# One PSUM tile per bank, mixing in halves, and a new order in an attention and feed-forward kernel

## The chip, the cores and the metric

The kernel runs on one core of a Trainium2 chip. The metric is the device time of one execution in microseconds (us), here as the median of the timed runs. A core has TensorE (PE, matrix products, with its weight loads in a row of their own, PEld), VectorE (DVE), ScalarE (ACT), GpSimd (POOL) and SyncE (SP, which issues every DMA of this kernel). Matrix products are written to PSUM, which has eight banks of 512 float32 columns on 128 partitions; DVE and ACT read them from there.

## The reference, cut to what matters

```python
def _attn_ref(q, k, v):                       # q, k, v: (8, 12, 448, 64) float32
    S = q.shape[2]
    scores = matmul(q, k.transpose(0, 1, 3, 2)) / sqrt(64) - log(S)
    attn = 1 / (1 + exp(-scores))             # sigmoid attention, no row sum
    return matmul(attn, v)

def _moe_ref(x, U, V, w_ch1, w_ch2):          # x: (8, 448, 768); U: (448, 32); V: (32, 448)
    h = x.transpose(0, 2, 1) @ U @ V          # mixing along the sequence, rank 32
    u = x + h.transpose(0, 2, 1)
    return u + maximum(u @ w_ch1, 0) @ w_ch2  # w_ch1: (768, 3072); w_ch2: (3072, 768)
```

The 12 heads of 64 features side by side make the 768 columns of `x`. U, V and both weights arrive as 64-bit words that the kernel decodes itself.

## The kernel before, in words

**Data.** Everything is kept with features on partitions. A batch of `x` or `u` is six tiles of 128 x 448, one for each pair of heads: `ua0..5` or `ub0..5` in the profile's names. A matrix product that must be exact to float32 is made of three float16 products: each operand is scaled and split into a high and a low half, and high*high, high*low and low*high are added up in one bank.

**Attention** (`pair`). For batches 0 and 1 it is done in float32, for 2 to 7 in split float16. A pair of heads has four key blocks (the numbers 3, 0, 1, 2; block 3 is half a block for each head). `scores_of` (L500) makes the scores of two blocks at a time; ACT takes the sigmoid (L587), then writes the high half (L610); DVE makes the low half (the helper `rest`, L358); `values_of` (L511, L515) multiplies by v; ACT evacuates the result to `ub` (L616), and `largest` (L421) takes its largest value for the next scale. Ahead of each pair its q, k and v are loaded, their bounds taken on ACT (L415) and spread by two small DMAs (`far`, `row`).

**Mixing** (`mix`). After its six pairs a batch is mixed. For batches 2 to 7 all six tiles get one scale (`scale_max`, with two small products on PE, L371 and L377), are split into the tile `us` (ACT and POOL the high, DVE the low halves), turned by two transposing DMAs into `xt` (L664), multiplied by U (L673, seven products for three tiles), evacuated by ACT and DVE to the tile `xnt` (L648 and L358), multiplied by V (L728, six products), and added to `ub` by DVE. Then the six tiles are stored to DRAM (`parked`), and the next batch of attention may overwrite `ub`.

**Feed-forward.** Batches 0 to 3 go through it plainly, in six groups of 512 hidden columns. `ffn_in` (L823) is a chain of 18 products, which ACT evacuates twice (L830 to `r`, L831 to `h`) and DVE once more (L832, low half). `ffn_out` (L843) is a chain of 12 products, whose sum DVE adds to `ua` (L358). Weights are decoded in the first batch (`decode`: DVE passes over the words, ACT bounds, ACT or POOL high halves, DVE low halves; for the last quarter of the weights of all groups but the first, the low half is made by ACT and POOL instead, L791 and L792) and kept in DRAM (`scratch`); later batches load them. Attention of the later batches is laid between these chains. Batches 4 to 7 go through it in two pairs at the end (L1016), with seven products of quarter blocks in place of eight: `in_quad` and `out_quad`, twelve of each for a pair of batches, 63 products each, in the order that the string `ORDER` gives. The sums of weight quarters for it are made on POOL all along (L902, L906).

**Order.** Nothing is scheduled on the chip. `Plan.op` collects each operation with its engine, its assumed cost, a due time (`pos`) and the tiles it reads and writes. `Plan.order` runs a list of events over them: whichever engine is free first takes the operation with the earliest due time among those that can start. The instructions are emitted in that order, each engine runs its own in that order, and the layer below sets semaphores between them. The due times hang on the tuned numbers at the top of the file. SP issues its DMAs in order too; each takes the next of eight semaphores.

**PSUM.** The banks are made as four tiles of two banks each; the plan gives them out bank by bank, and scores as whole tiles:

```python
BANKS = [Buffer(ps.tile([P, 2, 512], F32, name=f"banks{i}")) for i in range(4)]
BANK = [Buffer(x.ap[:, i]) for x in BANKS for i in range(2)]
PF, PS_ = [BANK[:4]] + [BANK[:3]] * (B - 1), [BANK[4:]] * 2 + [BANK[3:]] * (B - 2)
```

`PF[b]` are the banks of the feed-forward of batch b and of the small products of the scales, `PS_[b]` those of attention and mixing of batch b. So from batch 1 on the feed-forward has banks 0 to 2, and from batch 2 on attention and mixing have banks 3 to 7. Banks 2 and 3 are the two halves of the tile `banks1`.

## Time and profile before

| | |
|---|---|
| median of 3 runs | 1673.56 us (1671.91 to 1676.96) |
| profiled execution, time and span | 1673.21 us, 1671.4 us |
| PE busy | 1576.5 us (94%) |
| DVE busy | 1121.8 us (67%) |
| ACT busy | 837.9 us (50%) |
| POOL busy | 402.4 us (24%) |
| DMA | 322.52 MB, mean 193 GB/s |

The span runs from the first to the last instruction; the time has 1.8 us more around it. Busy times are sums without overlap. PE's is that of matrix products; its idle time is the rest of the span. In rows of the timeline, the bracket at the end gives the engine's idle time just before the row and the instruction that ended it. Names lose their buffer number in the profile, so that `banks` is any of the four PSUM tiles.

### The profile page before, as it was taken

Reading aid. Unit: us, or ns where it says so; the run is one execution under the profiler, and the core shown is the slowest. Engines: PE = TensorE matmul, PEld = TensorE weight load, DVE = VectorE, ACT = ScalarE, POOL = GpSimd, SP = SyncE. Lnnn points to the kernel's source line nnn. Section 1 sums busy time; section 2 is a strip of 40 time slices with the busy share of each in tenths; the row PEclk is TensorE's granted clock in tenths of the full one; section 3 lists DMA queues with packets and bytes.
Section 4 is the critical chain, followed back from the end, with each engine's and each line's share of the span. In section 5 each row is a group of like instructions: output and inputs, shape, how many; then the busy total and the mean of one; then the engine's idle time right before and its main releaser. Section 6 shows DMA issues by size and latency. Waiting matters only on the chain.

```text
span 1671.4 us, 23667 instructions
## 1 busy us (share of the span) xinstructions
PE 1576.5 (94%) x8756; PEld 768.8 (46%) x8756; DVE 1121.8 (67%) x1829; ACT 837.9 (50%) x1431; POOL 402.4 (24%) x484
## 2 busy tenths in 40 slices
PE   8989998999989999989979999999899999999998
PEld 3344444444444444444434444445455544545554
DVE  3788787666765566656657775685869687464745
ACT  6757665568647547737748765132324344130310
POOL 0100103542213443211312210065656150000000
PEclk9999999999999999999989999999999999999999
DMA  8698877675765777574665746986667574333321
GB/s 253 231 296 269 277 261 228 227 232 137 176 177 147 213 228 201 135 217 136 158 167 164 191 158 202 266 253 207 212 205 234 226 254 150 125 107 104 127 100 66
DMA packets 217428, 322.52 MB, mean 193 GB/s; under 512 B 132832, under 2 KB 183392, under 8 KB 205024
## 3 DMA queue, kind: packets, MB, share of 16 engines
q1 hardware_dynamic: 217312, 321.01, 61.9%
q8 instruction: 68, 1.11, 0.3%
q14 instruction: 48, 0.39, 0.1%
HBM read 249.40 MB, written 77.42 MB: 196 GB/s over the span
## 4 chain that ended last, share of the span: by engine, by line
PE 71%; DVE 12%; issue 5%; DMA 5%; ACT 4%; POOL 2%; SPq 1%; DVEq 0%; POOLq 0%; ACTq 0%
PE banks L1016 30%; PE banks L823 14%; PE banks L843 14%; PE banks L500 6%; PE banks L515 4%; PE banks L511 2%; DVE a L358 1%; DVE stg__109 L358 1%; DVE us__87 L358 1%; DMA w<-w_in 1%; DMA y_out<-ua__79 1%; POOL stg__109 L355 1%; SPq L335 1%; ACT junk L415 1%; ACT at L587 1%
## 5 line engine op out<-in xcount | busy, mean ns | idle before, releaser
L843 PE MATMUL banks<-h__93,w__91 128*128 128x448 f16 x864 | 176.8, 358 | 14.2 <-ACT ub__81 L616 8.5
L843 PE MATMUL banks<-h__94,w__92 128*128 128x448 f16 x864 | 176.4, 358 | 9.0 <-ACT r__96 L830 2.8
L358 DVE SCALAR_TENSOR_TENSOR a<-at,a 128x896 f16<-128x896 f32 (+1 forms) x145 | 143.1, 1009 | 50.6 <-ACT a L610 50.3
L823 PE MATMUL banks<-us__87,w__89 128*128 128x448 f16 x648 | 129.9, 356 | 8.0 <-ACT r__95 L830 2.8
L843 PEld LDWEIGHTS <-w__91 128*128 128x128 f16 x864 | 83.0, 99 | 102.6 <-issue 31.6
L823 PE MATMUL banks<-us__87,w__90 128*128 128x448 f16 x648 | 127.5, 353 | 1.8 <-ACT inv_x__199 L384 1.1
L843 PEld LDWEIGHTS <-w__92 128*128 128x128 f16 x864 | 83.2, 99 | 95.1 <-issue 23.6
L823 PEld LDWEIGHTS <-w__89 128*128 128x128 f16 x864 | 83.6, 98 | 92.9 <-issue 18.1
L823 PEld LDWEIGHTS <-w__90 128*128 128x128 f16 x864 | 83.0, 98 | 86.6 <-issue 10.7
L610 ACT ACTIVATE a<-at 128x896 f16<-128x896 f32 (+1 forms) x144 | 116.9, 851 | 0.5
L1016 PEld LDWEIGHTS <-w__89 128*128 128x128 f16 x819 | 80.1, 98 | 76.7 <-issue 2.1
L1016 PEld LDWEIGHTS <-w__91 128*128 128x128 f16 x756 | 73.9, 98 | 76.3 <-issue 8.0
L1016 PEld LDWEIGHTS <-w__90 128*128 128x128 f16 x756 | 73.9, 98 | 74.5 <-issue 6.2
L906 POOL TENSOR_TENSOR w<-w 128x384 f32<-128x384 f32 x96 | 105.3, 1097 | 5.9
L1016 PEld LDWEIGHTS <-w__92 128*128 128x128 f16 x693 | 68.2, 98 | 72.5 <-issue 11.0
L902 POOL TENSOR_TENSOR w<-w 128x384 f32<-128x384 f16 x64 | 67.0, 1063 | 124.9 <-DVE xnt L910 76.2
L909 ACT CAST xnt<-w 128x1536 f16<-128x1536 f32 x24 | 35.3, 1469 | 64.6 <-POOL w L906 60.3
L587 ACT ACTIVATE at<-banks,bias_s,c__221 128x896 f32<-128x896 f32 (+1 forms) x60 | 56.0, 947 | 16.5 <-DVE a L358 9.7
L587 ACT ACTIVATE at<-banks,bias_s,c__222 128x896 f32<-128x896 f32 (+1 forms) x60 | 56.1, 946 | 8.4 <-PE banks L500 6.9
L587 ACT ACTIVATE at<-banks,bias_s,c__220 128x896 f32<-128x896 f32 (+1 forms) x60 | 55.7, 946 | 5.3 <-PE banks L500 4.7
L830 ACT ACTIVATE r__96<-banks 128x448 f32<-128x448 f32 x48 | 26.0, 542 | 60.2 <-PE banks L823 24.3
L830 ACT ACTIVATE r__95<-banks 128x448 f32<-128x448 f32 x48 | 26.0, 541 | 55.4 <-PE banks L823 29.6
(1194 smaller groups left out, 3152.6 us busy)
## 6 DMA issues: line engine op xcount, KB each, us to landing
w<-w_in SPq DMA_DIRECT2D x48, 768.0 KB, 5.7
forms<-xnt SPq DMA_DIRECT2D x24, 768.0 KB, 4.4
w__89<-forms SPq DMA_DIRECT2D x13, 1344.0 KB, 6.4
w__90<-forms SPq DMA_DIRECT2D x12, 1344.0 KB, 5.9
w__91<-forms SPq DMA_DIRECT2D x12, 1344.0 KB, 6.0
w__92<-forms SPq DMA_DIRECT2D x11, 1344.0 KB, 5.9
forms<-scratch SPq DMA_DIRECT2D x144, 96.0 KB, 4.1
w__89<-scratch SPq DMA_DIRECT2D x9, 1536.0 KB, 7.3
```

Source lines behind the costliest of these rows:

```text
L358: nc.vector.scalar_tensor_tensor(out=out, in0=in0, scalar=s, in1=in1, op0=op0, op1=op1)
L500: nc.tensor.matmul(o, keys, y[rows_of(h)], start=i == 0, stop=i == n - 1)
L515: nc.tensor.matmul(av.x[rows_of(h), :S], x[:, j, rows_of(h)], y(tiles[j], h), start=False, stop=j == 2 and i == n - 1, skip_group_check=True,)
L587: act(cost, lambda: nc.scalar.activation(out_(), in_(), AF.Sigmoid, bias=bias_s[rows], scale=c if whole else c.x[rows]), kin + ["bias"] + ...
L610: act(0.57 if j == 3 else 0.95, lambda a=a, to=to: nc.scalar.activation(half(a, 0), to.x, AF.Copy, scale=A_UP), kto, [(a, 0)], here)
L823: nc.tensor.matmul(ph.x[:, :S], wx[:, x, c, f * P : (f + 1) * P], us.x[:, c, y, :], start=c == 0 and i == 0, stop=c == NP - 1 and i == 2,)
L830: act(0.54, lambda: nc.scalar.activation(r.x, ph.x[:, :S], AF.Relu, scale=DOWN_H), [ph], [r], pos - 4)
L843: nc.tensor.matmul(po.x[:, :S], wx[:, x, f, e * P : (e + 1) * P], h.x[:, f, y, :], start=f == 0 and i == 0, stop=f == FC - 1 and i == 2,)
L902: pool(1.0, lambda j=j: nc.gpsimd.tensor_tensor(out=t.x[:, j], in0=quarter(j, 0), in1=quarter(j, 1), op=ALU.add), [(w, j, 0), (w, j, 1)] i ...
L906: pool(1.0, lambda o_=o_, x=x, y=y, sub=sub: nc.gpsimd.tensor_tensor(out=t.x[:, o_], in0=t.x[:, x], in1=t.x[:, y], op=ALU.subtract if sub ...
L909: act(1.45, lambda: nc.scalar.copy(o.x[:, :, :, 0], t.x.rearrange(order)), [(t, j) for j in range(4)], [(o, 0)], pos)
L1016: nc.tensor.matmul(bank.x[:, :S], wt.x[:, k, FACTOR[n], x], both(f)[:, y], start=start and k == i == 0, stop=k == 2 and i == 2, skip_group ...
```

## The change

Nine things are changed. (1) PSUM is eight tiles of one bank. (2) The scores of a block take two of these tiles, one for each head, from all the banks of attention (before: a two-bank tile of `banks2` or `banks3`, for all but the first pairs), and each gets a sigmoid of its own: two of 448 columns where one of 896 stood. (3) Batches 2 to 7 are mixed in halves of three tiles by the new function `mix_half`, one half after the third pair and one after the sixth, each with its own scale, its own tile `xs` for the split halves (before: one of the two `us` tiles that the feed-forward reads too) and its own `th` (before: a half of one `xnt` tile); there is one `xt` tile in place of two, and the stores to `parked` of three tiles follow each half. (4) `Plan.order` lets a DMA start only when the one eight before it has landed. (5) `LOW_POOL` is empty: the low halves that ACT and POOL made in `decode` are made by DVE. (6) `largest` of batch 1 is on DVE, no longer on ACT. (7) `ORDER` has in and out alternating. (8) The far sums of `far_forms` use seven places, four of them others. (9) All tuned numbers are new, among them `EV_IN` and `EV_OUT`: evacuations of the feed-forward are due 21.3 and 5.6 us ahead of their chains where both had 4.

The program has the same matrix products but for 12 small ones of the scales (8548 for 8536), 58 more DVE instructions (1889 for 1831), 134 more on ACT (1399 for 1265), 16 fewer on POOL (470 for 486) and as many DMAs.

```diff
-LOW_POOL = (3,)
-MIXED1, MIX_1 = 6.58, 6.69
...
-ORDER = "iiiioooiiioooiiioooiiooo"
+LOW_POOL = ()
+MIXED1, MIX_1 = 6.47, 3.6
+MIX_2, EV_IN, EV_OUT, A_OFF = 1.824, 21.322, 5.63, 0.0
...
+ORDER = "iiiioiooiioiooiioiooiooo"
...
-        done, port = [], 0.0
+        done, port, landed = [], 0.0, [0.0] * 8
...
-   now.append((max(free[e], ready[i], r[0] + o[5] if r[1] else 0.0, port if o[8] else 0.0), o[4], i))
+   now.append((max(free[e], ready[i], r[0] + o[5] if r[1] else 0.0, port if o[8] else 0.0, landed[-8] if e == "SP" else 0.0), o[4], i))
...
+            if e == "SP":
+                landed.append(end[i] + o[6])
...
-    XT = [Buffer(w64h[:, i * NP * S : (i + 1) * NP * S].rearrange("p (n d) -> p n d", d=P)) for i in range(2)]
+    XT = [Buffer(w64h[:, : NP * S].rearrange("p (n d) -> p n d", d=P))]
+    XS = [Buffer(w64h[:, NP * S : 2 * NP * S].rearrange("p (c x s) -> p c x s", c=3, x=2))]
...
+    TH = [Buffer(xnt[:, NP * P + i * 192 : NP * P + (i + 1) * 192].bitcast(F16)) for i in range(2)]
...
-    BANKS = [Buffer(ps.tile([P, 2, 512], F32, name=f"banks{i}")) for i in range(4)]
-    BANK = [Buffer(x.ap[:, i]) for x in BANKS for i in range(2)]
...
+    BANK = [Buffer(ps.tile([P, 512], F32, name=f"bank{i}")) for i in range(8)]
     PF, PS_ = [BANK[:4]] + [BANK[:3]] * (B - 1), [BANK[4:]] * 2 + [BANK[3:]] * (B - 2)
...
-        sc = {j: plan.tile("sc", BANKS if early else BANKS[2:], False) for j in js}
+        sc = {(j, h): plan.tile("sc", BANK if early else PS_[b], False) for j in js for h in range(2)}
...
+            for h in range(2):
+                rows = rows_of(h) if j == 3 else slice(0, P)
+                cols = slice(0, S) if j == 3 else slice(h * S, h * S + S)
+                sigmoid(0.66 if whole else 0.72, lambda to=to, rows=rows, cols=cols: to.x[rows, cols],
+                        lambda h=h, sc=sc, j=j, rows=rows: sc[j, h].x[rows, :S], rows, here, [sc[j, h]], [(to, h)])
...
-            largest(lambda: u32[p].x, lambda: mx.x[:, p : p + 1], [ku], (mx, p), late, b == 1)
+            largest(lambda: u32[p].x, lambda: mx.x[:, p : p + 1], [ku], (mx, p), late)
...
+    def mix_half(b, hf, pos):
+        u32, mx, cs = u32s[b], mxs[b], range(3 * hf, 3 * hf + 3)
+        sx, ix = scale_max(mx, [(mx, c) for c in cs], "x", pos, cols=slice(3 * hf, 3 * hf + 3))
+        kap = sm("kap", 1)
+        dve(0.2, lambda: nc.vector.tensor_mul(kap.x, ix.x, puv), [ix, "puv"], [kap], pos)
+        xs, xt = plan.tile("xs", XS), plan.tile("xt", XT)
+        for c in cs:
+            i = c % 3
+            if i == 1:
+                pool(0.75, lambda c=c, i=i: scaled(xs.x[:, i, 0], u32[c].x, sx.x), ...)
+            else:
+                act(0.65, lambda c=c, i=i: nc.scalar.activation(xs.x[:, i, 0], u32[c].x, AF.Copy, scale=sx.x), ...)
+            dve2(0.63, lambda c=c, i=i: rest(xs.x[:, i, 1], u32[c].x, sx.x, xs.x[:, i, 0]), ...)
+        op("SP", 1.0, lambda: nc.sync.dma_start_transpose(out=xt.x, in_=xs.x.rearrange("p c x s -> p (c x s)")), ...)
+        tp, tt = plan.tile("av", PS_[b], False), plan.tile("th", TH)
...
+        pe(1.2, mixed, [xt, "ux"] + KUA, [tp], pos + 2.0)
+        act(0.5, lambda: nc.scalar.activation(tt.x, tp.x[:, :384], AF.Copy, scale=DOWN), [tp], [tt], pos + 2.0)
+        dve(0.55, lambda: rest(tt.x[32:64], tp.x[32:64, :384], DOWN, tt.x[32:64]), [tp, tt], [tt], pos + 2.0)
+        at = pos + MIX_2
+        for c in cs:
...
+            lp = plan.tile("sc", PS_[b], False)
+            pe(MM, lambda lp=lp, cut=cut: nc.tensor.matmul(lp.x[:, :S], tt.x[:, cut], vst, start=True, stop=True), ...)
+            dve(0.68, lambda lp=lp, c=c: stt(u32[c].x, lp.x[:, :S], kap.x, u32[c].x, ALU.mult, ALU.add), ...)
+            largest(lambda c=c: u32[c].x, lambda c=c: mx.x[:, c : c + 1], [u32[c]], (mx, c), at)
+            load(lambda c=c: parked[b][:, c], lambda c=c: u32[c].x, P * S * 4, [u32[c]], [("parked", b, c)], at + 1.0)
...
-        act(0.54, ... AF.Relu, scale=DOWN_H), [ph], [r], pos - 4)          # and the same for h and its low half
+        act(0.54, ... AF.Relu, scale=DOWN_H), [ph], [r], pos - EV_IN)
...
-            [po, (kg, g), ku], [ku], pos - 4)
+            [po, (kg, g), ku], [ku], pos - EV_OUT)
...
-            return plan.tile("uw", SPOT[-10:-4])
+            return plan.tile("uw", SPOT[-4:] + SPOT[-10:-7])
...
+            if b >= WHOLE and p % 3 == 2:
+                mix_half(b, p // 3, start + (MIXED - 5 + p) * d)
+        if b < WHOLE:
+            mix(b, 0.0, start + MIXED1 * d)
```

How the change moves instructions is shown at three places, first as the rows stood and then as they stand.

On ACT, in the feed-forward of batch 3, with attention of a later batch between its chains. `r` and `h` are evacuations of the feed-forward, `at` those of scores, `ub` those of attention's values, `c` and `cv` scales; the number behind `banks` or `bank` is the tile's. Before:

```order
L831 ACTIVATE h1__94<-banks1_111 128x448
L830 ACTIVATE r0__95<-banks1_111 128x448
L587 ACTIVATE at_98<-banks3_113,bias_s_65,c1__221 128x896
L587 ACTIVATE at_98<-banks2_112,bias_s_65,c1__221 128x896
L610 ACTIVATE a_97<-at_98 128x896 x2
L648 ACTIVATE xnt_106<-banks3_113 128x384 x2
L909 CAST xnt_106<-w64_107 128x12x128
L616 ACTIVATE ub0__81<-banks1_111,cv0__223 128x448
L830 ACTIVATE r1__96<-banks0_110 128x448
L831 ACTIVATE h1__94<-banks0_110 128x448
```

Now, at a like place:

```order
L611 ACTIVATE a_97<-at_98 128x896
L420 ACTIVATE junk_74,ss2__214<-qk2__101 128x448
L617 ACTIVATE ub1__82<-bank6_116,cv1__228 128x448
L420 ACTIVATE junk_74,ss2__214<-qk2__101 128x448
L420 ACTIVATE junk_74,ss0__212<-v2__104 128x512
L845 ACTIVATE r0__95<-bank1_111 128x448
L846 ACTIVATE h1__94<-bank1_111 128x448
L590 ACTIVATE at_98<-bank3_113,bias_s_65,c2__226 128x448
L590 ACTIVATE at_98<-bank6_116,bias_s_65,c2__226 128x448
```

A feed-forward chain and attention's values, both in halves of `banks1` before, have tiles of their own now, and each sigmoid of 896 columns from a two-bank tile has become two of 448 from two tiles.

On SP, where the last tiles of batch 2 leave (`y_out`), those of batch 3 are loaded to `ua`, and the mixed tiles of batch 5 are stored to `parked`. Before:

```order
L335 DMA v__104<-v_in 128x512
L335 DMA y_out<-ua__79 128x448
L335 DMA y_out<-ua__80 128x448
L335 DMA far_2_119<-ss__210 128x3
L335 DMA ua__79<-parked_122 128x448
L335 DMA parked_124<-ub__81 128x448
L335 DMA parked_124<-ub__82 128x448
L335 DMA ua__80<-parked_122 128x448
L335 DMA parked_124<-ub__83 128x448
L335 DMA parked_124<-ub__84 128x448
```

Now:

```order
L340 DMA row__120<-far_1_122 128x384
L340 DMA far_2_123<-ss__214 128x3
L340 DMA parked_128<-ub__81 128x448
L340 DMA parked_128<-ub__82 128x448
L340 DMA parked_128<-ub__83 128x448
L340 DMA qk__99<-k_in 64x448
L340 DMA qk__99<-q_in 64x448
```

The stores of the first three tiles stood behind `y_out<-ua__79`; now they stand 26 rows ahead of it, and those of the other three 11 rows behind it.

On PE, where the third of the late batches is mixed: L673 (now L755) is the product with U, L728 (now L764) that with V, which reads `xnt` after ACT and DVE have evacuated the first. Before:

```order
L673 LDWEIGHTS vraw
L673 MATMUL banks_113<-w_107,vraw 128x384
L728 LDWEIGHTS xnt
L728 MATMUL banks_113<-vst,xnt 128x448
L728 LDWEIGHTS xnt
L728 MATMUL banks_112<-vst,xnt 128x448
L843 LDWEIGHTS w__92
```

Now, at the first half of that batch; the last row of L755 stands 49 rows further up, ahead of two feed-forward chains of 12:

```order
L858 LDWEIGHTS w__91
L858 MATMUL bank_112<-h__93,w__91 128x448
L764 LDWEIGHTS xnt
L764 MATMUL bank_117<-vst,xnt 128x448
L764 LDWEIGHTS xnt
L764 MATMUL bank_116<-vst,xnt 128x448
L764 LDWEIGHTS xnt
L764 MATMUL bank_113<-vst,xnt 128x448
```

The product with V stood straight behind that with U; now two chains stand between them.

More of the change, by code (lines that the diff above doesn't have):

```diff
@@ L274, in fused_kernel @@
     WO = [Buffer(xnt.bitcast(F16).rearrange("p (a n x b) -> p a n x b", a=3, n=4, x=2))]
-    for x in XN + T:
+    TH = [Buffer(xnt[:, NP * P + i * 192 : NP * P + (i + 1) * 192].bitcast(F16)) for i in range(2)]
+    for x in XN + T + TH:
         WO[0].shares.append(x)
         x.shares.append(WO[0])
+    for x in TH:
+        T[0].shares.append(x)
+        x.shares.append(T[0])
     STG = ring("stg", 2, [4 * PIECE], F16)
@@ L500, in fn @@
                         nc.tensor.matmul(o, keys, y[rows_of(h)], start=i == 0, stop=i == n - 1)
-        pe(len(js) * (4 if b < WHOLE else 3) * MM + 0.2, fn, kp, [(t, h) for t in sc.values() for h in range(2)], pos, after=values_ops[-2:-1])
+        pe(len(js) * (4 if b < WHOLE else 3) * MM + 0.2, fn, kp, list(sc.values()), pos, after=values_ops[-2:-1])
         return sc
@@ L609, in pair @@
                 continue
-            act(0.57 if j == 3 else 0.95, lambda a=a, to=to: nc.scalar.activation(half(a, 0), to.x, AF.Copy, scale=A_UP), kto, [(a, 0)], here)
-            dve2(0.63 if j == 3 else 1.16, lambda a=a, to=to: rest(half(a, 1), to.x, A_UP, half(a, 0)), kto + [(a, 0)], [(a, 1)], here)
+            act(0.57 if j == 3 else 0.95, lambda a=a, to=to: nc.scalar.activation(half(a, 0), to.x, AF.Copy, scale=A_UP), kto, [(a, 0)], here + A_OFF)
+            dve2(0.63 if j == 3 else 1.16, lambda a=a, to=to: rest(half(a, 1), to.x, A_UP, half(a, 0)), kto + [(a, 0)], [(a, 1)], here + A_OFF)
             keys += [(a, 0), (a, 1)]
@@ L736, in mix, with u_parts @@
                 load(lambda c=c: parked[b][:, c], lambda c=c: u32[c].x, P * S * 4, [ku[c]], [("parked", b, c)], at + 1.0)
-        if b >= PLAIN:
-            return
+        u_parts(b, at)
+    def u_parts(b, at):
+        u32, mx = u32s[b], mxs[b]
+        ku, kmx = u32, [(mx, c) for c in range(NP)]
         su, iu = scale_max(mx, kmx, "u", at)
-        if b < 2:
-            uss[b] = plan.tile("us", US)
-        us = uss[b]
+        us = uss[b] = plan.tile("us", US)
         for c in range(NP):
@@ L754, in fused_kernel, with mixed @@
     kgs, ius = {}, {}
-    def scale_max(mx, kmx, name, pos, top=TOP):
+    def mix_half(b, hf, pos):
[7 more added lines that the diff above has]
+            if i == 1:
+                pool(0.75, lambda c=c, i=i: scaled(xs.x[:, i, 0], u32[c].x, sx.x), [u32[c], sx], [(xs, i, 0)], pos)
+            else:
+                act(0.65, lambda c=c, i=i: nc.scalar.activation(xs.x[:, i, 0], u32[c].x, AF.Copy, scale=sx.x), [u32[c], sx], [(xs, i, 0)], pos)
+            dve2(0.63, lambda c=c, i=i: rest(xs.x[:, i, 1], u32[c].x, sx.x, xs.x[:, i, 0]), [u32[c], sx, (xs, i, 0)], [(xs, i, 1)], pos)
+        op("SP", 1.0, lambda: nc.sync.dma_start_transpose(out=xt.x, in_=xs.x.rearrange("p c x s -> p (c x s)")),
+           [(xs, i, x) for i in range(3) for x in range(2)], [xt], pos + 1.0, land=7.0)
+        tp, tt = plan.tile("av", PS_[b], False), plan.tile("th", TH)
+        def mixed():
+            x = xt.x.rearrange("p (c j) d -> p j c d", c=3)
+            for j in range(7):
+                m = ua[:, j] if j < 3 else ux[:, j - 3]
+                nc.tensor.matmul(tp.x[:, :384], m.rearrange("p a b -> p (a b)"), x[:, j], start=j == 0, stop=j == 6)
+        pe(1.2, mixed, [xt, "ux"] + KUA, [tp], pos + 2.0)
[3 more added lines that the diff above has]
+        for c in cs:
+            cut = slice((c % 3) * P, (c % 3 + 1) * P)
+            lp = plan.tile("sc", PS_[b], False)
+            pe(MM, lambda lp=lp, cut=cut: nc.tensor.matmul(lp.x[:, :S], tt.x[:, cut], vst, start=True, stop=True), [tt, "vst"], [lp], at)
+            dve(0.68, lambda lp=lp, c=c: stt(u32[c].x, lp.x[:, :S], kap.x, u32[c].x, ALU.mult, ALU.add), [lp, u32[c], kap], [u32[c]], at)
+            largest(lambda c=c: u32[c].x, lambda c=c: mx.x[:, c : c + 1], [u32[c]], (mx, c), at)
+            load(lambda c=c: parked[b][:, c], lambda c=c: u32[c].x, P * S * 4, [u32[c]], [("parked", b, c)], at + 1.0)
+        if hf and b < PLAIN:
+            u_parts(b, at + 0.5)
@@ L758, in scale_max @@
+    def scale_max(mx, kmx, name, pos, top=TOP, cols=slice(None)):
         mm = sm(f"mm_{name}", 1)
-        dve(0.2, lambda: nc.vector.tensor_reduce(out=mm.x, in_=mx.x, axis=AX.X, op=ALU.max), kmx, [mm], pos)
+        dve(0.2, lambda: nc.vector.tensor_reduce(out=mm.x, in_=mx.x[:, cols], axis=AX.X, op=ALU.max), kmx, [mm], pos)
         return scale_of(mm, [mm], 1, name, pos, top)
```

70 lines of the change are left out of this document (17 added, 53 removed).

## The prediction

> **What bounds the kernel.** I read the page first (busy shares, then the chain that ended last), then the stages one by one, then PE's idle pieces in the timeline, each with what ended it.
>
> ```profile
> span 1671.4 us, 23667 instructions
> PE 1576.5 (94%) x8756; PEld 768.8 (46%) x8756; DVE 1121.8 (67%) x1829; ACT 837.9 (50%) x1431; POOL 402.4 (24%) x484
> PE 71%; DVE 12%; issue 5%; DMA 5%; ACT 4%; POOL 2%; SPq 1%; DVEq 0%; POOLq 0%; ACTq 0%
> ...
> 0.00:85.70 85.70, 79.12 (x320) 27.78 (x320) 48.96 (x96) 57.30 (x93) 11.54 (x21) 1.00 0.80 247
> 85.70:295.70 210.00, 192.29 (x981) 93.52 (x980) 166.64 (x301) 131.84 (x257) 29.80 (x29) 0.98 0.81 265
> 295.70:535.50 239.80, 229.85 (x1410) 110.88 (x1409) 154.76 (x249) 154.10 (x257) 75.33 (x105) 0.99 0.60 178
> 786.60:1053.10 266.50, 247.81 (x1535) 119.57 (x1534) 179.02 (x305) 172.82 (x289) 45.39 (x76) 0.98 0.62 176
> 1053.10:1225.10 172.00, 162.13 (x842) 82.47 (x840) 129.03 (x183) 52.71 (x82) 82.88 (x78) 0.99 0.74 232
> 1225.10:1671.40 446.30, 431.77 (x2269) 221.64 (x2267) 287.71 (x446) 122.95 (x210) 76.94 (x69) 1.00 0.45 154
> ```
>
> PE is the bound in every stage but for its gaps. The rows of stages (PE, PEld, DVE, ACT, POOL busy; clock; DMA share) are: before the first feed-forward chain, batch 0 with the decoding, batch 1, batch 3, the first half of the first pair of late batches, and the rest. The change leaves PE's products as they are, so what it can win is idle time: 1671.4 - 1576.5 = 94.9 us, and the time that slow clocks cost. I went through PE's idle pieces and set beside each the instruction that ended it.
>
> ```profile
> 115.76 0.27 PE L371 MATMUL banks<-ident,mm_w__181 128*1 128x128 f32 x1 [1.50 <-DVE ua__76 L358]
> 479.69 0.54 PE L823 MATMUL banks<-us__87,w__89 128*128 128x448 f16 x2 [2.61 <-ACT r__95 L830]
> 569.22 4.03 PE L843 MATMUL banks<-h__94,w__92 128*128 128x448 f16 x12 [2.80 <-ACT r__96 L830]
> 725.12 0.93 PE L728 MATMUL banks<-vst,xnt 128*128 128x448 f16 x2 [5.45 <-DVE xnt L358]
> 857.31 4.27 PE L843 MATMUL banks<-h__93,w__91 128*128 128x448 f16 x11 [8.47 <-ACT ub__81 L616]
> 932.66 0.73 PE L511 MATMUL banks<-a,stg__109 128*128 128x448 f16 x3 [1.38 <-DVE ua__79 L358]
> 1200.44 2.33 PE L1016 MATMUL banks<-a,w__92 128*128 128x448 f16 x6 [2.16 <-DVE at L358]
> 1204.40 1.30 PE L1016 MATMUL banks<-at,w__92 128*128 128x448 f16 x6
> 1393.81 0.73 PE L1016 MATMUL banks<-stg__109,w__92 128*128 128x448 f16 x3 [0.78 <-DVE a L358]
> 1655.07 0.73 PE L1016 MATMUL banks<-qk__99,w__91 128*128 128x448 f16 x3 [0.33 <-DVE ua__76 L358]
> ...
> 1393.07 0.68 DVE L358 SCALAR_TENSOR_TENSOR a<-banks,fg,us__88 128x448 f32<-128x448 f32 x1 [2.16 <-PE banks L1016]
> ```
>
> At 857.31 a feed-forward chain (L843) waits 8.47 us for ACT to evacuate attention's values (L616); at 932.66 attention's values (L511) wait for DVE's addition to `ua`. These two kinds of work never share a bank: the feed-forward has banks 0 to 2, attention 3 to 7. They share a tile, `banks1`. So the built program makes PE wait for the reader of the tile's other bank. By the banks that the code gives to both sides, 41 pieces (first 115.76, last 1655.07) of 44.2 us in sum are such crossing waits. Readers wait likewise: at 1393.07 DVE waits 2.16 us until PE has finished the partner bank, though its own was full a product earlier, and PE's next product then waits 0.78 us for DVE, a true wait that a crossing one made. The plan knew of neither.
>
> **The change part by part.** *Crossing waits.* With one tile per bank they cannot arise. Bounds: 0 (each is followed at once by a true wait) to -44.2 us. How much returns is nearest to the true waits for the right bank that stand beside them now:
>
> ```profile
> 84.00 1.40 PE L500 MATMUL banks<-qk__101 64*128 64x448 f32 x6 [0.63 <-ACT a L587]
> ...
> 1644.36 0.73 PE L1016 MATMUL banks<-qk__99,w__92 128*128 128x448 f16 x3 [0.78 <-DVE ub__84 L358]
> ...
> PEld L728 <- DVE xnt L358: 6.9, 3, 5.8
> ```
>
> They are 23 pieces (these two the first and the last) with 18.0 us in sum, 0.8 each; if 14 of the 41 left as much behind, 11 us would return. So I take three quarters of the sum: -33.
>
> *Their second order in the tail.* Pieces of 0.78 us like that at 1393.81 stand eight times after 1300 (the last at 1644.36): -6. Alternating in and out changes no instruction; DVE is busy 287.7 of 446.3 us there and covers it: 0.
>
> *Mixing in halves.* At 725.12 PE waited 5.45 us for `xnt`, since the product with V stood straight behind that with U. Waits of this kind sum to 6.9 us in three pieces (the row L728 above). In the new order at least 2.4 us of other products stand between the two in all twelve halves, mostly 3.4 to 5.7: -6, bounds 0 and -7. The stores that follow each half matter for 857.31:
>
> ```profile
> 856.63 0.64 ACT L616 ACTIVATE ub__81<-banks,cv__223 128x448 f32<-128x448 f32 x1 [5.54 <-DMA parked<-ub__81]
> ...
> 841.93 8.91 DMA y_out<-ua__79
> 851.27 5.27 DMA parked<-ub__81
> ```
>
> ACT could not write `ub__81` before its store had landed, which had queued on SP behind `y_out`. With three stores 26 rows further up the queue this goes in any case (counted above). The price is six more scales: two PE products of 0.27 and 0.35 us each with a wait behind them (558.70 below has 0.88), so 6 x (0.62 + 0.9) = +9 at most, 0 at least; I take +3, since in the new order one to two chains stand between the two products, as before.
>
> ```profile
> 430.75 0.38 PE L377 MATMUL banks<-e_x__197,ones 1*128 1x1 f32 x2
> 436.43 3.32 SPq L664 DMA_TRANSPOSE w<-us__88  x1
> 449.78 0.65 PE L673 MATMUL banks<-w,ua 128*128 128x384 f16 x3
> 558.70 0.35 PE L377 MATMUL banks<-e_x__198,ones 1*128 1x1 f32 x2 [0.88 <-DVE e_x__198 L355]
> 577.14 9.17 SPq L664 DMA_TRANSPOSE w<-us__87  x2
> ...
> DMA to landing us min/median/max: 5.0/5.6/10.7
>   PE banks L673: 0.4, 1
> ```
>
> From the scale to the landed transpose it took 436.43 - 430.75 + 5.6 = 11 us at one mixing, 577.14 - 558.70 + 5.6 = 24 at another; PE came to the product only 19 and 35 us after the scale, and all twelve products waited 0.4 us together. Counted in products at their durations here, the new order leaves 12.5 to 23 us in eleven halves. Half as many splits stand ahead of the transpose: 0, with the rival below. `xs` is no longer a tile that feed-forward chains read: no wait goes, none comes.
>
> *Sigmoids, decoding, maxima.*
>
> ```profile
> L587 ACT ACTIVATE at<-banks,bias_s,c__222 128x896 f32<-128x896 f32 x36 | 38.8, 1097 | 2.8 <-PE banks L500 1.7 <-DVE a L358 0.8
> L587 ACT ACTIVATE at<-banks,bias_s,c__220 64x448 f32<-64x448 f32 x24 | 17.3, 720 | 4.3 <-PE banks L500 4.1
> L792 POOL TENSOR_TENSOR w__90<-stg__109,w__90 128x768 f16<-128x768 f32 x1 | 1.8, 1834 | 27.1 <-ACT stg__109 L791 27.1
> L358 DVE SCALAR_TENSOR_TENSOR w__90<-us__88,s_w__190,w__90 128x768 f16<-128x768 f32 x3 | 2.9, 1010 | 0.0
> L421 DVE TENSOR_REDUCE mx__162<-ub__81 x2: 611/616/620, 350.0 to 458.8; 128x1 f32<-128x448 f32 x2
> ```
>
> Two sigmoids of 448 columns (720 each, by the row of the half block) for one of 896 (1097): +0.34 us x 108 = +37 us of ACT, spread over batches 1 to 3. ACT is busy 154 to 173 of 240 to 267 us there and goes to some 70%; each bank is free after its own half. Bounds 0 and +8; I take +2. Decoding: ten low halves of 1.01 us and twelve maxima of 0.62 go to DVE, +17.5 us, nearly all in 85.7:295.7, where DVE is busy 166.6 of 210 us, the fullest DVE of any long stage; POOL is rid of ten that took 1.6 to 3.1 us. PE waits for those weights, and chains queue behind them. Bounds: 0 (covered by DVE's 43 idle us) and +17.5; I take +5.
>
> *Clock.* Behind 2.16 us of idle time six products took 2.33 us (1200.44), where six take 1.30 (1204.40); behind 8.47 us eleven took 4.27 (857.31), behind 2.80 us twelve took 4.03 (569.22). Six gaps of over 2 us (2.16, 2.61, 2.80, 4.97, 5.45, 8.47) ran so, some 1.8 us dearer each: 11 us. Four of them are crossing waits, one is the wait for `xnt`: at three quarters -7. [...]
>
> *The plan.* Eight running DMAs in the plan, the new due times and `far_forms`' places add no instruction. What they win or lose is order, which I don't price apart from the above: 0.
>
> Sum: -33 - 6 - 6 + 3 + 2 + 5 - 7 = -42. The profiled execution took 1673.21 us, 1.8 around its span and 0.35 below the median: 1631.
>
> **Rivals.**
> 1. *The transposes come late* (slower). A half's product with U stands in PE's queue, and everything behind it waits. If the chain from scale to landing took 24 us, as at 558.70, against a cover of about 16 on the mean, twelve halves would cost 12 x 8 = 96: 1631 + 96 = 1727. It decides from 42 / 12 = 3.5 us of wait per half. For it: SP held a transpose for 9.17 us. Against: 0.4 us in all before, and stores and loads of `ua` that held SP up stand apart now.
> 2. *DVE becomes the bound of the decoding.* If its 43 idle us there stay, since it waits for others in them, batch 0 takes 17.5 us longer than now, not 5, and four gaps of that make cost 1.8 each by the clock: 12.5 + 7 = 20, so 1651. For it: DVE ran 79% there with passes of about 1 us that evacuations queue behind. Against: part of those waits are crossing ones.
> 3. *Crossing waits turn into true ones.* DVE and ACT are late anyhow and PE waits for the right bank instead: of -33 and -6 a third remains, 13, and of the clock's -7 another 2: 1631 + 26 + 5 = 1662. For it: true waits of 18 us stand beside the crossing ones. Against: the readers' own waits on partner banks go too.
> 4. *Nearly all idle time goes*, because the plan's picture of the program is now true: a further 20 of the remaining some 45 us: 1611.
>
> **Numbers.** Chances: forecast 0.46, rival 1 0.09, rival 2 0.16, rival 3 0.14, rival 4 0.15. The range, 1604 to 1666, reaches from below rival 4 to past rival 3; left out are rival 1, the upper end of rival 3 and what lies under 1604. No change means within 0.3% (about 5 us, what a measurement of this kernel can tell). Slower: 0.07, from rival 1; same: 0.06, from the weak ends of rivals 1 and 3; faster: 0.87.
>
> **What would show it.** PE's idle sum falls to about 50 us with 1577 - 8 busy; no feed-forward row waits for L616's successor, and no attention row for an addition to `ua`; products with V wait under 3 us together; the half-clock stretches after 400 us are one or two. Wrong would be: waits of products with U for the transposing DMA above 20 us in sum (rival 1), the stage of batch 0 above 225 us with DVE over 90% busy (rival 2), or as many waits for `r`, `h` and `ua` as now (rival 3).

## The result, and the profile after

| | before | after |
|---|---|---|
| median | 1672.74 us (1671.35 to 1676.96) | 1600.66 us (1595.18 to 1601.40) |
| profiled execution, time and span | 1673.21, 1671.4 us | 1600.42, 1598.6 us |
| PE busy, idle in the span | 1576.5, 94.9 us | 1563.9, 34.7 us |

Both kernels were timed in four runs each. The ratio is 0.956, 95% interval [0.953, 0.959]: 72 us faster where 42 were forecast, outside the range (1604 to 1666). From the page of after come the busy times and the chain that ended last; below them are the stages in the columns of the prediction's rows: batch 0, batch 1, batch 3, the first and the second half of the first late pair, the last pair.

```profile
span 1598.6 us, 23902 instructions
PE 1563.9 (98%) x8774; PEld 769.3 (48%) x8774; DVE 1163.3 (73%) x1887; ACT 855.8 (54%) x1553; POOL 385.4 (24%) x468
PE 82%; DVE 9%; DMA 4%; ACT 2%; SPq 1%; issue 1%; POOL 1%; ACTq 0%; DVEq 0%; POOLq 0%
...
85.00:290.20 205.20, 200.53 (x1037) 99.11 (x1036) 187.37 (x343) 124.57 (x245) 18.04 (x26) 0.99 0.86 286
290.20:504.00 213.80, 213.80 (x1323) 104.17 (x1322) 143.54 (x231) 146.89 (x269) 69.98 (x94) 1.00 0.62 180
739.10:985.50 246.40, 246.40 (x1552) 120.13 (x1551) 184.90 (x322) 185.16 (x336) 44.18 (x74) 1.00 0.67 193
985.50:1153.00 167.50, 159.29 (x832) 81.59 (x830) 132.66 (x175) 55.33 (x86) 88.30 (x80) 0.99 0.74 234
1153.00:1308.80 155.80, 145.33 (x758) 74.40 (x757) 126.40 (x160) 51.97 (x86) 75.29 (x66) 0.99 0.65 219
1308.80:1598.00 289.20, 286.18 (x1513) 147.84 (x1511) 172.97 (x286) 66.88 (x120) 0.00 (x0) 1.00 0.34 119
```

PE has no idle time at all in batches 1 and 3 and 0.5 us in batch 2 (46.2 us in the three before). What is left stands in the first 290 us, in the first late pair (8.2 + 10.5 us, where before had 9.9 + 3.8), and 3.0 at the end. The list of PE's waits in after (line, what it waited for, us in all, times, longest) says for what:

```profile
PE bank L1031 <- DVE ub__84 L363: 9.3, 4, 3.0
PE bank L503 <- DMA qk__99<-q_in: 4.1, 1, 4.1
PE bank L1031 <- DVE a L363: 3.1, 1, 3.1
PE bank L1031 <- DVE h__94 L360: 2.0, 1, 2.0
PE bank L1031 <- DMA at<-ufar: 1.8, 1, 1.8
```

No feed-forward row waits for attention's evacuation (L617 now), no attention row for an addition to `ua`. The products of the late pair (L1031) wait for DVE more than before, which the third group of runs takes up.

I sorted PE's idle pieces over 0.05 us by what ended them, for each trace in the same way: a reader of the other bank of the tile (crossing), or a true one (the right bank, or an operand in SBUF).

| kernel | span | crossing | right bank | operand | PE busy | half clock |
|---|---|---|---|---|---|---|
| before | 1671.4 | 44.2 in 41 | 18.0 | 22.3 | 1576.5 | 34.1 |
| e1, tiles alone | 1605.8 | 0 | 19.5 | 11.9 | 1566.6 | 23.9 |
| after | 1598.6 | 0 | 16.5 | 8.7 | 1563.9 | 13.6 |
| e3, after with pairs | 1705.9 | 59.5 in 53 | 28.4 | 21.3 | 1588.6 | 40.9 |
| e5, one shared pair | 1616.9 | 18.1 in 10 | 14.4 | 11.7 | 1564.1 | 17.1 |
| e6, the other three | 1651.3 | 25.2 in 35 | 25.8 | 20.0 | 1570.0 | 23.9 |
| e15, turns with POOL | 1589.4 | 0 | 5.6 | 7.7 | 1561.1 | 6.8 |

Waits for a DMA are in none of these columns: 6.1 us in before, 4.2 in e1, 5.9 in after and 11.5 in e15, of which some 4 us stand at the start of each. The last column is the time inside the span at a granted clock of one half, without the stretch that the span's end cuts. In after, groups of three products of 128x448 begin 1.11 and 1.13 us apart in such stretches (at 1086.56 and at 1287.89) and 0.57 us apart just behind them, so half of the time at half clock is taken for lost below: an estimate.

### The profile page after: what moved, and what is told of

Read it like the earlier page. It is cut to its first block, busy times and chain, and to the rows that moved or that the text cites. A ratio compares the mean times of both kernels' runs of the same rounds, so it can differ in the third digit from the quotient of the medians.

```text
span 1598.6 us, 23902 instructions
## 1 busy us (share of the span) xinstructions
PE 1563.9 (98%) x8774; PEld 769.3 (48%) x8774; DVE 1163.3 (73%) x1887; ACT 855.8 (54%) x1553; POOL 385.4 (24%) x468
## 3 DMA queue, kind: packets, MB, share of 16 engines
q8 instruction: 68, 1.11, 0.3%
## 4 chain that ended last, share of the span: by engine, by line
PE 82%; DVE 9%; DMA 4%; ACT 2%; SPq 1%; issue 1%; POOL 1%; ACTq 0%; DVEq 0%; POOLq 0%
PE bank L1031 28%; PE bank L838 18%; PE bank L858 18%; PE bank L503 8%; PE bank L518 5%; PE bank L514 2%; DVE us__88 L363 1%; DMA qk__99<-q_in 1%; DVE xnt L925 1%; DVE us__87 L1069 1%; PE bank L755 1%; SPq L747 1%; DMA forms<-xnt 1%; DMA far<-ss__213 1%; DVE h__94 L363 1%
## 5 line engine op out<-in xcount | busy, mean ns | idle before, releaser
L858 PE MATMUL bank<-h__94,w__92 128*128 128x448 f16 x864 | 173.1, 353 | 1.4 <-DVE a L363 0.9
L858 PE MATMUL bank<-h__93,w__91 128*128 128x448 f16 x864 | 173.1, 353 | 0.0
L611 ACT ACTIVATE a<-at 128x896 f16<-128x896 f32 (+1 forms) x144 | 123.1, 855 | 0.5
L1031 PEld LDWEIGHTS <-w__89 128*128 128x128 f16 x819 | 80.1, 98 | 80.0 <-issue 5.4
L921 POOL TENSOR_TENSOR w<-w 128x384 f32<-128x384 f32 x96 | 110.4, 1150 | 5.2
L1031 PEld LDWEIGHTS <-w__91 128*128 128x128 f16 x756 | 74.4, 98 | 74.5 <-issue 6.4
L1031 PEld LDWEIGHTS <-w__90 128*128 128x128 f16 x756 | 73.9, 98 | 73.7 <-issue 5.0
L1031 PEld LDWEIGHTS <-w__92 128*128 128x128 f16 x693 | 68.3, 99 | 69.5 <-issue 7.3
L838 PE MATMUL bank<-us__87,w__90 128*128 128x448 f16 x432 | 86.5, 357 | 0.9 <-DVE ua__78 L363 0.9
L838 PE MATMUL bank<-us__87,w__89 128*128 128x448 f16 x432 | 85.0, 353 | 1.2 <-ACT h__93 L846 1.2
L838 PE MATMUL bank<-us__88,w__90 128*128 128x448 f16 x432 | 85.8, 353 | 0.0
L838 PE MATMUL bank<-us__88,w__89 128*128 128x448 f16 x432 | 85.6, 353 | 0.0
L590 ACT ACTIVATE at<-bank,bias_s,c__226 128x448 f32<-128x448 f32 (+1 forms) x96 | 67.0, 725 | 14.9 <-PE bank L503 11.2
L590 ACT ACTIVATE at<-bank,bias_s,c__224 128x448 f32<-128x448 f32 (+1 forms) x96 | 66.8, 724 | 8.0 <-PE bank L503 5.2
L590 ACT ACTIVATE at<-bank,bias_s,c__225 128x448 f32<-128x448 f32 (+1 forms) x96 | 66.3, 721 | 4.6 <-PE bank L503 2.5
L590 ACT ACTIVATE a<-bank,bias_s 128x448 f32<-128x448 f32 (+1 forms) x96 | 55.9, 630 | 10.7 <-PE bank L503 10.1
```

Source lines behind the costliest of these rows:

```text
L590: act(cost, lambda: nc.scalar.activation(out_(), in_(), AF.Sigmoid, bias=bias_s[rows], scale=c if whole else c.x[rows]), kin + ["bias"] + ...
L611: act(0.57 if j == 3 else 0.95, lambda a=a, to=to: nc.scalar.activation(half(a, 0), to.x, AF.Copy, scale=A_UP), kto, [(a, 0)], here + A_OFF)
L838: nc.tensor.matmul(ph.x[:, :S], wx[:, x, c, f * P : (f + 1) * P], us.x[:, c, y, :], start=c == 0 and i == 0, stop=c == NP - 1 and i == 2,)
L858: nc.tensor.matmul(po.x[:, :S], wx[:, x, f, e * P : (e + 1) * P], h.x[:, f, y, :], start=f == 0 and i == 0, stop=f == FC - 1 and i == 2,)
L921: pool(1.0, lambda o_=o_, x=x, y=y, sub=sub: nc.gpsimd.tensor_tensor(out=t.x[:, o_], in0=t.x[:, x], in1=t.x[:, y], op=ALU.subtract if sub ...
L1031: nc.tensor.matmul(bank.x[:, :S], wt.x[:, k, FACTOR[n], x], both(f)[:, y], start=start and k == i == 0, stop=k == 2 and i == 2, skip_group ...
```

## The experiments

### The tiles, all and one at a time

e1 is before with eight one-bank tiles and nothing else new but that a sigmoid is issued as two; e2 has only the two sigmoids; e3 is after with its banks back in pairs.

```diff
e1 (on before)
-    BANKS = [Buffer(ps.tile([P, 2, 512], F32, name=f"banks{i}")) for i in range(4)]
-    BANK = [Buffer(x.ap[:, i]) for x in BANKS for i in range(2)]
+    BANK = [Buffer(ps.tile([P, 512], F32, name=f"bank{i}")) for i in range(8)]
+    BANKS = [Buffer([BANK[2 * i].ap, BANK[2 * i + 1].ap]) for i in range(4)]
e1 and e2 (on before; in e2 the input is sc[j].x[:, h, :S])
+                def two(to=to, sc=sc, j=j):
+                    for h in range(2):
+                        nc.scalar.activation(to.x[:, h * S : h * S + S], sc[j].x[h][:, :S], AF.Sigmoid, ...)
e3 (on after)
+    PAIRS = [ps.tile([P, 2, 512], F32, name=f"banks{i}") for i in range(4)]
+    BANK = [Buffer(x[:, i]) for x in PAIRS for i in range(2)]
```

> The kernel before in its own order, every instruction in its old place, but with eight one-bank tiles; since one ACT instruction can't read two tiles, each 896-column sigmoid is issued as two of 448 in the same place. Theory A (crossing waits are the main loss): the 44 us of crossing waits, the waits of 0.78 us they made in the tail (6) and some 7 us of slow clock go, little comes back: 1673 - 50 = 1615 to 1630 us. Rival B (the new order is the main gain, the tiles a small one): true waits take the crossing ones' place, 1650 to 1665 us.

> The kernel before in its own order with two-bank tiles, only each 896-column sigmoid issued as two of 448: the price of the split by itself, 46 us of ACT. Theory A: ACT has room, 0 to +5 us (1672 to 1678). Rival (ACT's evacuations are late already, and each 0.34 us counts where chains wait behind them): +8 to +20 us.

> The changed kernel in its own order, every instruction in its place, but PSUM is again four tiles of two banks, so that crossing waits are back. Theory A: the time goes back by 45 us or more, and since banks of attention are now given out singly, by more crossing pairs than before: 1645 to 1690 us. Rival B: the new order keeps most of its gain, 1605 to 1625 us.

Measured: e1 1603.2 us, ratio 0.960 [0.958, 0.962]; e2 1673.5, 1.001 [0.9998, 1.003]; e3 1713.3, 1.027 [1.025, 1.030]. The tiles alone give nearly all of it, the two sigmoids cost nothing that can be told, and the new order on paired banks is 113 us slower than after. Theory A names the right cause and is too small on both sides: e1 lies 12 us under its range, e3 23 us over it. From before to e1 every engine runs the same order. By the table the span falls by 65.6: 44.2 of crossing waits, 8.9 of true waits, 9.9 of busy time (5 of it, by the estimate, for the 10.2 us of half clock that go), and 2.6 of small ones and DMAs (e1's profiled execution, 1607.6 us, lies 4.4 above its median). Nothing came back as true waits. The lines of busy times from the pages of e1 and of e3:

```profile
PE 1566.6 (98%) x8756; PEld 769.2 (48%) x8756; DVE 1127.2 (70%) x1829; ACT 864.9 (54%) x1575; POOL 410.4 (26%) x484
...
PE 1588.6 (93%) x8774; PEld 773.3 (45%) x8774; DVE 1156.5 (68%) x1887; ACT 854.8 (50%) x1553; POOL 387.1 (23%) x468
```

PE's products are the same but for the small ones of the scales; e3 has 22 us more of busy PE than e1, at 17 us more of half clock, which by the estimate explain 8.5 of them; the rest is not taken apart. What the readers lose is in none of these lines: in before, DVE waited 225.6 us (110 pieces) and ACT 177.2 us (67) until PE had finished the partner bank, sigmoids that read both banks not counted; in e3 it is 238.7 and 197.3, in e1 and after 0. So the evacuations themselves came late in before, and the true waits beside the crossing ones were partly of their making. e5 and e6 split the tiles: in e5 only banks 2 and 3, which feed-forward and attention share, are one tile; in e6 they alone are apart.

```diff
e5 (on e1)
+    two = ps.tile([P, 2, 512], F32, name="banks1")
+    BANK = [Buffer(two[:, i - 2] if i in (2, 3) else ps.tile([P, 512], F32, ...)) for i in range(8)]
e6 (on e1)
+    PAIRS = {i: ps.tile([P, 2, 512], F32, name=f"banks{i}") for i in (0, 2, 3)}
+    BANK = [Buffer(ps.tile([P, 512], F32, ...) if i in (2, 3) else PAIRS[i // 2][:, i % 2]) for i in range(8)]
```

> The kernel of one tile per bank in the order of before (1603.2 us), with banks 2 and 3 alone put back into one tile, the one that feed-forward and attention share from batch 2 on. In before 13 of the 41 crossing pieces of PE, 20.7 of 44.2 us, lie in that tile. Theory A (each tile costs in proportion to its crossing waits on PE, followers included): 20.7 / 44.2 of the 70 us that all tiles were worth, so 1603 + 33 = 1636 us, with some 20 us of crossing waits back in this tile alone. Theory B (the waits of the readers inside one kind of work, score pairs and feed-forward chains, carry the rest, and the shared tile is a small part): under 1615. Theory C (crossing waits replace one another, whichever tile is left): over 1650.

> The complement: banks 2 and 3 are tiles of their own, the other six banks stay three two-bank tiles, order of before, sigmoids in two. Theory A (in proportion): 70 x 20.7 / 44.2 = 33 us faster than before, 1640. Theory B (the other tiles carry it): over 1658. Theory C (crossing waits replace one another): within 5 us of before, 1668 to 1678, with the crossing waits of the other tiles above the 23.5 us that they had.

Measured: e5 1620.9, 0.971 [0.968, 0.974], 18 us above e1; e6 1654.2, 0.991 [0.989, 0.994], 51 above e1. None of the three theories gave both numbers; B, by which the other tiles carry most, is nearest, and C falls, since 18 and 51 add up to the 70 that all four tiles are worth. The shared tile costs as much as its crossing waits on PE (18.1 us, 7.40 of it the old wait for `ub__81`), the other three twice theirs (25.2 us). Against e1, e6 has 25.2 us of crossing waits, 14.4 more of true ones and 3.4 more of busy time, 43.0 of the 45.5 us between the spans. Rows of the timeline of e5 (PE, ACT) and of e6 (DVE, PE) show the two kinds:

```profile
822.23 2.02 PE L847 MATMUL banks<-h__93,w__91 128*128 128x448 f16 x5 [7.40 <-ACT ub__81 L620]
821.55 0.63 ACT L620 ACTIVATE ub__81<-banks,cv__226 128x448 f32<-128x448 f32 x1 [5.26 <-DMA parked<-ub__81]
...
1389.59 0.68 DVE L359 SCALAR_TENSOR_TENSOR stg__108<-banks,fg,r__96 128x448 f32<-128x448 f32 x1 [1.91 <-PE banks L1020]
1390.33 0.73 PE L1020 MATMUL banks<-v__104,w__91 128*128 128x448 f16 x3 [0.78 <-DVE stg__108 L359]
```

In e5 a chain waits for work of another kind. In e6 DVE waits 1.91 us for PE to fill the partner bank, and PE then 0.78 us for DVE: a true wait by its label, which is gone in e1 and in after. Seven of the eight such pieces that before had in the tail stand in e6.

### The other parts, taken out of after one at a time

```diff
e4   ORDER = "iiiioooiiioooiiioooiiooo"                        # in and out as before
e8   mix(b, 0.0, start + (MIXED1 if b < WHOLE else MIXED) * d)  # before's whole mix for late batches
e9   no landed[-8] in Plan.order
e10  SUMS, STEP_K, STEP_I = 0.61, 21.88, 9.86                   # POOL's sums due as before
e11  LOW_POOL = (3,)                                            # last low halves on ACT and POOL again
```

> The changed kernel with the old string ORDER (three in, three out) and all else as changed. Theory A has alternating as worth nothing: PE's seven waits of 1.5 to 3.2 us for DVE between 1065 and 1287 us (16 us in sum) come from the new string or from the DVE work beside it, and the old string gives 1588 to 1603 us. Rival (alternating spreads DVE's work of the in products and is a part of the gain): 1605 to 1615 us.

> The changed kernel with the late batches mixed whole again, as before: one scale for six tiles, U and V products in a row, stores at the end; all else as changed. The prediction's terms for halves: -6 (waits for xnt) and +3 (six scales), so 1600.7 + 3 = 1604 us, with three waits for xnt of some 5 us in sum in batches 1 to 3. Rival (the retuned order needs the halves: without them batches 1 to 3 fall back to the idle time that one tile per bank alone left there, 15 us): 1612 to 1620. Rival (halves are worth nothing): 1598 to 1602.

> The changed kernel without the plan's limit of eight running DMAs, so that the plan starts a DMA as soon as SP is free, as before; all numbers as changed. The prediction's term for the plan: 0, so 1598 to 1603 us. Rival (the limit is what makes the plan's picture true, and without it PE waits for loads and transposes): 1608 or more, with PE's waits for DMAs above the 1.8 us that they have in the changed kernel.

> The changed kernel with the due times of the weight sums on POOL in the first pair of late batches as before (SUMS, STEP_K, STEP_I 0.61, 21.88, 9.86 for 18.57, 22.57, 8.637). In the changed kernel PE waits for DVE there in eight pieces of 0.86 to 3.15 us, 18.7 us of idle time in the two halves against 7.6 with one tile per bank alone. Theory (DVE is late because its passes over SBUF take 1.33 to 1.41 us beside POOL's sums against 0.61 without, and the new due times put them beside the passes that an evacuation queues behind): 1588 to 1594 us, idle time of the two halves below 12. Rival (it is the order of DVE's own work, or of the quads): 1598 to 1603. Rival (the old due times are worse now): over 1604.

> The changed kernel with the low halves of the last quarter of the weights made by ACT and POOL again, as before (LOW_POOL = (3,)); the maxima stay on DVE. Theory (decoding on DVE costs some 10 us in whatever order, as it did in the order of before): 1590 to 1595 us, the stage of batch 0 back from 205 to 200. Rival (the new due times are made for it, so that DVE's passes are hidden there and POOL's would be late): 1601 to 1612. The prediction's term (+5 for decoding and maxima together): 1596 to 1598.

| | median us | ratio to before, 95% |
|---|---|---|
| after | 1600.7 | 0.956 [0.953, 0.959] |
| e4 | 1601.7 | 0.959 [0.957, 0.961] |
| e8 | 1610.2 | 0.965 [0.963, 0.967] |
| e9 | 1615.5 | 0.965 [0.963, 0.967] |
| e10 | 1614.1 | 0.964 [0.962, 0.966] |
| e11 | 1619.9 | 0.969 [0.967, 0.970] |

Only ORDER is worth nothing, as predicted. Each of the others costs 10 to 19 us when undone (e8 by 10, where the prediction's terms had 3 and its rival 11 to 19), and my theories for e10 and e11 are refuted: old due times for the sums raise the first pair's idle time from 18.7 to 30.0 us, and with POOL decoding again batch 0 took 210 us, not 200. In e11 PE waits for `xnt` in batch 1's mixing and then for an addition; in e9 the products with V wait again, and not, as the rival had it, PE for DMAs:

```profile
249.45 0.47 PE L684 MATMUL bank<-xnt,ub 64*128 64x384 f16 x1 [7.56 <-DVE xnt L363]
275.09 3.14 PE L838 MATMUL bank<-us__87,w__90 128*128 128x448 f16 x8 [7.99 <-DVE ua__75 L363]
...
692.38 1.30 PE L764 MATMUL bank<-vst,xnt 128*128 128x448 f16 x3 [4.96 <-DVE xnt L363]
```

The waits come at other places than the part undone: the whole order moved. The converse is to put parts alone on e1, in the order of before: e7 the decoding and maxima on DVE, e12 the limit of eight DMAs, e14 the halves (with MIXED 6.5), e13 both.

```diff
e7   LOW_POOL = ()  and  largest always on DVE
e12  landed[-8] if e == "SP" else 0.0   in Plan.order, as in after
e13  e12 with mix_half, XS, TH of after; MIX_2 = 1.824
e14  mix_half, XS, TH of after; MIX_2 = 1.824, MIXED = 6.5
```

> One tile per bank in the order of before, plus the change's decoding alone: the last low halves and the maxima of batch 1 on DVE. The prediction's term: +5, so 1608 us. Its rival 2 (DVE becomes the bound of the decoding): +12.5 and the clock, 1616 to 1623, with the stage of batch 0 (199.5 us with one tile per bank) 12 us longer or more and DVE over 90% busy in it. Cover (the 30 us in which DVE is idle there take it all): 1601 to 1605.

> One tile per bank in the order of before (1603.2 us), with the plan's limit of eight running DMAs. Set theory (a part is worth something only with the due times tuned for it, and any new order undoes what tuning had found): 1603 or slower, up to 1620. Part theory (the limit is worth some 15 us by itself, as its loss from the changed kernel was): 1586 to 1593. The prediction's term: 0, 1601 to 1606.

> One tile per bank in the order of before, with mixing in halves and the limit of eight running DMAs, at the due times of before (MIX_2 alone, which before has not, is 1.824 as in the changed kernel). Part theory: 1575 to 1585 (15 for the limit, 9 for halves). The prediction's terms (-6 + 3 + 0): 1600. Set theory: 1600 to 1620, the waits for xnt of batches 2 and 3 gone (5.3 us) and others in their place.

> The same without the limit, and with the halves' due time MIXED at 6.5 in place of 5.79. Part theory: 1592 to 1596. The prediction's terms: 1600. Set theory: 1600 to 1620. A wait that must show if the halves do what the prediction said: none for xnt in batches 2 to 7.

Measured (e1: 0.960 [0.958, 0.962]): e7 1612.8, 0.968 [0.963, 0.972]; e12 1628.9, 0.976 [0.973, 0.978]; e13 1650.5, 0.989 [0.987, 0.991]; e14 1651.6, 0.991 [0.988, 0.993]. All are slower than e1, by 10 to 48 us (13 to 51 by the ratios, which also allow for before's median of 1668 to 1674 us from one group of runs to another), and e12 to e14 by more than the set theory allowed, though in e14 the waits for `xnt` of late batches fell from 5.3 to 2.3 us. In e7 evacuations queue behind passes of the decoding and maxima, as rival 2 had it. This profile is of e7's slowest run, 1626.7 us, 14 above the median: batch 0 took 210.5 us in it, against 199.5 in e1, with DVE busy 89%, just short of both signs that rival 2 named. In rows of DVE, then PE:

```profile
271.60 0.95 DVE L358 SCALAR_TENSOR_TENSOR stg__109<-w,stg__109 128x768 int32<-128x768 int32 x1
272.47 0.15 DVE L762 TENSOR_REDUCE mm_u__168<-mx__165 128x1 f32<-128x6 f32 x1
272.54 0.68 DVE L358 SCALAR_TENSOR_TENSOR ua__79<-bank,kg__179,ua__79 128x448 f32<-128x448 f32 x1
273.27 2.02 PE L826 MATMUL bank<-us__87,w__90 128*128 128x448 f16 x5 [6.08 <-DVE ua__79 L358]
```

So none of these parts shows a worth of its own: at the due times of after, undoing one costs 10 us or more, and at those of before, or near them, adding one costs 10 us or more. The whole set is 2.5 us better than e1 by medians (7 by the ratios, whose intervals overlap). That small sum hides a gain and a loss: PE's idle time in batches 1 to 3 is 15.4 us in e1 and 0.5 in after, in the first late pair 7.6 and 18.7. Which due time does what was not taken apart.

### The wait that the change brought, and a faster version

After's longest wait in the late pair, in rows of DVE, POOL and PE:

```profile
1194.69 1.33 DVE L363 SCALAR_TENSOR_TENSOR us__88<-a,h__94 128x448 f32<-128x448 f32 x1
1199.70 1.41 DVE L1069 TENSOR_TENSOR r__95<-us__87,r__95 128x448 f16<-128x448 f32 x1
1201.04 1.41 DVE L363 SCALAR_TENSOR_TENSOR us__88<-us__88,us__87 128x448 f32<-128x448 f32 x1
1202.37 0.67 DVE L363 SCALAR_TENSOR_TENSOR at<-bank,fg,us__87 128x448 f32<-128x448 f32 x1
1203.16 0.69 DVE L363 SCALAR_TENSOR_TENSOR a<-bank,fg,at 128x448 f32<-128x448 f32 x1
1199.26 5.12 POOL L921 TENSOR_TENSOR w<-w 128x384 f32<-128x384 f32 x4
1203.90 1.30 PE L1031 MATMUL bank<-a,w__89 128*128 128x448 f16 x6 [3.15 <-DVE a L363]
```

Six passes of 1.33 to 1.41 us beside POOL's sums (such passes took 0.62 in after with POOL idle) stand ahead of the evacuation that PE waits for. The plan has a rule by which DVE's passes over two SBUF operands take turns with POOL, but `in_quad` issues its passes without it, at 0.68. e15 gives them the rule, e16 makes the splits due 8 us later instead, e17 does both, and e18 is e15 with the sums due 5 us earlier.

```diff
e15 (on after, five places of in_quad)
-                dve(0.68, lambda: nc.vector.tensor_tensor(out=o.x, in0=x.x, in1=y.x, op=ALU.subtract), [x, y], [o], pos)
+                dve2(0.68, lambda: nc.vector.tensor_tensor(out=o.x, in0=x.x, in1=y.x, op=ALU.subtract), [x, y], [o], pos)
e16 (on after, in split)
+            pos += 8
e18 (on e15)
-LEAD, SUMS, ... = 35.115, 18.57, ...
+LEAD, SUMS, ... = 35.115, 13.57, ...
```

> The changed kernel; in the plan, the five kinds of DVE passes over two SBUF operands of the late pairs' first product (in_quad) now take turns with POOL, as the passes elsewhere do; nothing else is changed, and only the order of the late pairs can move. Theory (the plan priced them wrong, and with the true picture evacuations come in time): idle time of the first pair 18.7 to under 10 us, 1588 to 1594. Rival (it is the order among due times on DVE): 1597 to 1604. Rival (POOL's sums come later in such an order, and PE waits for the weights made of them): over 1606.

> The changed kernel with the splits of in_quad (a copy on ACT and a pass on DVE each, needed only by a later quad) due 8 us later, so that evacuations of banks stand ahead of them on DVE. Theory (evacuations queue behind passes that nobody waits for yet): idle time of the first pair under 10 us, 1588 to 1594. Rival (the passes are late for out_quad then): PE waits for operands in SBUF in their place, 1600 to 1615.

> Both edits together. If each of the two accounts held a part of it: below either, 1585 to 1592. If the one makes the other useless: as the better of the two. If any shift of the tuned order costs, as in the runs before: 1605 to 1620.

> The kernel of e15 (1588.5 us) with the sums on POOL due 5 us earlier (SUMS 13.57). In e15 the longest wait of the first pair is 4.21 us at 1184 for weights made of these sums, loaded after SP issued at 1182.3; DVE no longer holds anything up there. Theory (the sums are now late by about those 4 us, and earlier ones come in time): 1583 to 1586, no wait for weights above 1 us. Rival (the passes on DVE pay for earlier sums): 1588 to 1594, waits for DVE back above 5 us in the first pair.

Measured: e15 1588.5, 0.951 [0.949, 0.953]; e16 1601.8, 0.959 [0.957, 0.961]; e17 1591.8, 0.953 [0.951, 0.955]; e18 1587.5, 0.951 [0.948, 0.953]. e15 beats both kernels, 12 us under after by the medians (after's interval begins where e15's ends, at 0.953). PE's idle time in the first late pair falls from 18.7 to 9.0 us, as the theory had it, and in batches 1 to 3 it stays at 0.3. Later due times alone (e16) do nothing, and beside the rule (e17) they add nothing. DVE's busy time falls by 21.3 us with the same passes, to 1142.0, and the waits for DVE in the first pair are nearly gone (e15's list of waits, then e18's):

```profile
PE bank L1031 <- DMA w__89<-forms: 4.2, 1, 4.2
PE bank L1031 <- DMA at<-ufar: 3.1, 1, 3.1
PE bank L1031 <- DVE ub__84 L363: 0.8, 1, 0.8
...
PE bank L1031 <- DMA w__89<-forms: 5.4, 1, 5.4
PE bank L1031 <- DMA at<-ufar: 1.6, 1, 1.6
```

What is late next are weights made of POOL's sums. Making them due earlier did not mend it (5.4 us for 4.2): that theory fell, DVE's waits did not come back either, and e18 is no different from e15.

## Why the prediction was right in direction and wrong in size

In the terms of the sum, from profile to profile (-72.8 us against -42):

- *Crossing waits, -33: the step that failed.* The bound of -44.2 was the measured value. "How much returns is nearest to the true waits" took those waits for the readers' own lateness. e6 shows that crossing waits on the readers' side make true waits; without them the true waits fell by 8.9 us in e1, where the prediction had 11 coming back. In after they fell by 15.1, 12 of which are the forecast of the next two terms. The prediction had seen this mechanism and priced it in the tail alone.
- *Second order in the tail, -6*: right. None of the eight pieces of 0.78 us is left.
- *Mixing, -6*: right in after, where the wait for `xnt` is 0.3 us in all; the tiles alone left 5.3 of it. No U product waits for a transpose: rival 1 fell.
- *Scales, sigmoids, decoding, +3, +2, +5*: none shows as idle time. Sigmoids alone are worth -0.3 to +4.5 us (e2's interval). Their ACT time was mis-sized: the prediction had 37 us for 108 sigmoids, but 144 are split, and ACT's busy time rose by 27.7 us (837.9 to 865.6 in e2). Batch 0 has DVE busy 187.4 of 205.2 us (91%), yet PE idle 4.7 us there against 17.7 before and 6.9 in e1. In e1's order the same decoding cost 10 us, so its price hangs on the order, not on DVE's share.
- *Clock, -7 of 11*: PE's busy time fell by 12.6 us; the 20.5 us of half clock that went are worth 10, by the estimate of half. Two half-clock stretches stand after 400 us, as forecast, beside the one that the span's end cuts.
- *The plan, 0*: wrong as a statement on its parts (e9 to e14), near right for their sum on top of the tiles, 2.5 to 7 us, but by luck: some 15 us won in batches 1 to 3 against 11 lost in the late pair.

The miss of 30.8 us is 11.2 of crossing waits that did not return, 10 of costs that were covered, 5.6 of busy time, and 4 of other waits. Rival 3 was the opposite of what happened, rival 4 (nearly all idle time goes, 1611) the nearest; its chance of 0.15 was too small, and even its price was 10 us too high.

## What to carry to other kernels

Count a wait for the wrong half of a tile on both sides: what the readers lose to it came back to the bound engine here as waits that look true (14.4 us more of them in e6). A part of a planned order need not have a price of its own; take it out of the new order and put it into the old one before believing either number. And where a planner lays the work, look for where its picture and the program differ (a shared tile, passes of DVE that took 1.33 to 1.41 us beside POOL where the plan had 0.68): both wins here, 70 us and 12 us, came from making the two agree.
